# Query loads of 128 rows, a planner that keeps two-input steps apart, narrow zero products and early branch hints in an mLSTM and MoE kernel on one core

## The chip, the cores and the metric

The kernel runs on one core of a Trainium2 chip. The core has five engines with a queue of instructions each, which wait for each other by semaphores: PE (TensorE, matrix products), DVE (VectorE), ACT (ScalarE), POOL (GpSimd) and SP (SyncE), and 16 DMA engines that move data between the chip's memory (HBM) and the core's (SBUF). The metric is the device time of one execution in microseconds (us).

## The reference

Two layers. The first is an mLSTM, a recurrence over 768 tokens for 4 batches and 8 heads of 40 elements; the second a mixture of experts that sends each of the 3072 tokens to one of 8 experts, by its data and its modality.

```python
for t in range(S):                                   # S = 768
    m_new = np.maximum(f_gate[:, :, t] + m, i_gate[:, :, t])
    f_stab, i_stab = np.exp(f_gate[:, :, t] + m - m_new), np.exp(i_gate[:, :, t] - m_new)
    C = f_stab * C + i_stab * outer(v_t, k_t);  n = f_stab * n + i_stab * k_t
    y[:, :, t] = sigmoid(o_gate_t) * (C @ q_t) / np.maximum(np.abs(n @ q_t), 1.0)
x = y as rows of 3072 tokens x 320
logits = x @ w_gate + modality_bias[modality_id]     # 320 x 8
e_idx, gate_w = argmax, its softmax probability
for e in range(8):
    h = np.maximum(x[mask] @ w1[e], 0.0)             # 320 x 1024
    out[mask] = gate_w * (h @ w2[e])                 # 1024 x 320
```

## The kernel before, in words

The kernel has two arms. The first (`still_arm`) assumes properties of the inputs that hold here: that the state of the recurrence is nearly still after the first tokens, and that nearly all tokens of a modality go to one expert. It checks them as it goes, and ends with a verdict (`bword`). A branch on it, L2534, either runs the second, general arm ("rest") or skips it; with these inputs it is skipped. All that follows is the first arm.

**Stages.** The first keys and values (kvs) give a state S for all heads. The 3072 tokens are 24 chunks of 128. For each chunk `light` makes the products S with the chunk's queries (qg), L1924, into the banks Y or H. A query load (`load_q`, L1697) brings two chunks, a gate load (`load_o`, og) the output gates of two. `token_rows` makes tokens of them: DVE multiplies by the gate (xr, L1940), the denominators (ab) follow on ACT, POOL or DVE, POOL divides (L1956), ACT casts the high halves, and DVE or POOL make the low halves (rows, L1610 and L1962). All float32 values are split into two float16 halves, high (h) and low (l), and a product is three products of halves. POOL then scatters the rows into a buffer in HBM, sorted by modality (x_s, L1977).

Two experts, A and B, get all tokens but odd ones. Their weights come in eight pieces each (`load_w`): the load into a stage buffer by SP, the high half by ACT, the low half by DVE (w1lA, w2lA, w1lB, w2lB, L1883). The sorted tokens are 15 tiles, 25 halves of 128 tokens, A and B in turn (`STREAM`). For a tile of two halves, `expert` makes four groups of 16 H products (L2179), which go round three banks (H_63, H_64, H_65); after each, ACT makes hh (the high half after the ReLU, L2184) and DVE hl (L2186), both from the bank. Then follow 24 O products a half (L2195): 16 from hh, 8 from hl. ACT scales them (ob, L2204) and POOL scatters them to the output (L2205). The first tiles' tokens are not taken from HBM but chosen from the rows by products with selection matrices (`select`, sel). `logits` computes the gate of each tile by the real data and finds tokens that go to another expert than their tile's. `odd_row` (L2220 and on) corrects one such token: a product of fs (the sums that tell where it lies) gives fl, from this come its row number fp_i and its expert fe_i; POOL gathers the row (xrow, L2239), SP loads that expert's whole weights into the stage and og buffers, and DVE computes the row by itself (xf, fjunk, facc). The last is summed by a product Y from facc, and scattered.

**What sets the order.** Everything in the arm is a task of `class Plan` (some 1080 tasks): an engine, a duration by formula, what it reads and writes. `plan.run` lays them out in time, each engine taking, of the tasks that are ready, the one with the least latest start time plus a bias; the table `NUDGE` adds a number to the bias of single tasks. A load's end is its issue, then its size by `DMA_KB` behind earlier loads, plus `DMA_FIRST`. The result is only an order: each engine issues its tasks in it, and waits by semaphore for what they need. `idle_products` puts products of a zero tile (zrow) into bank M0 where the plan leaves PE idle over 0.3 us, between 5 and 60 us of planned time.

The instructions of the arm are emitted in two pieces. Between them, on every engine, stands a hint on the branch to "rest", at present ahead of the last tile's O products (`found["cut"]`).

Of the kernel before, what the change touches and what calls it, by code (L numbers as in the profile page):

```python
# [10 lines left out]
F32 = mybir.dt.float32  # L11
# [19 lines left out]
class Plan:  # L31
# [5 lines left out]
    DMA_FIRST = 3.0  # L37
    DMA_KB = 320.0
# [9 lines left out]
    def add(self, eng, dur, fn, r=(), w=(), kb=None, nb=None, chain=None, bias=0.0, lat=0.0):  # L48
# [18 lines left out]
        self.tasks.append(dict(eng=eng, dur=dur, fn=fn, deps=deps, order=order, kb=kb, nb=nb, bias=bias + NUDGE.get(i, 0), lat=lat, early=self.early, w=list(w)))  # L67
# [5 lines left out]
    def run(self):  # L73
# [29 lines left out]
        dma_free = 0.0  # L103
        order, start, end = [], [0.0] * n, [0.0] * n
        while len(order) < n:
# [15 lines left out]
            t = ts[i]  # L121
            start[i] = s
            fin = s + t["dur"]
            e["free"] = fin
# [1408 lines left out]
NSTAGE = 7  # L1533
WARM = 10
FILL = (5.0, 60.0)
PRE = 4
SOON = 20.0
RING = 12
# [41 lines left out]
def still_arm(tc, a, out):  # L1580
# [60 lines left out]
    qg = [tl([120, 2, 3, P], F32, f"qg{i}") for i in range(3)]  # L1641
    qh, ql = ([tl([120, 2, 3, P], F16, f"q{n}{i}") for i in range(2)] for n in "hl")
# [54 lines left out]
    def load_q(i):  # L1697
        dma(368, lambda: sy.dma_start(qg[i % 3], a["ql"][:, 2 * i:2 * i + 2]), w=[f"qg{i % 3}"], bias=FIRST.get(f"q{i}", 0))
# [54 lines left out]
    for h in range(2):  # L1753
        sl = slice(FT * h, FT * h + FT)
        dve(140, lambda sl=sl: v.tensor_tensor_scan(m[:, sl], gf[:, sl], gi[:, sl], -1e30, ALU.add, ALU.max), r=["gs"], w=["m"])
    dve(128, lambda: tt(two(gt)[:, :, 1:], two(gf)[:, :, 1:], two(m)[:, :, 0:FT - 1], ALU.add), r=["gs", "m"], w=["gt"])
# [401 lines left out]
    def expert(k):  # L2158
# [29 lines left out]
        for h in range(nh):  # L2188
            no, op = take("O")
            seq = [(hh, w, f) for f in range(NFC) for w in (w2h, w2l)] + [(hl, w2h, f) for f in range(NFC)]  # L2190
            for q in range(0, 24, 4):
# [8 lines left out]
                if k == len(STREAM) - 1 and q == 0:  # L2200
                    found["cut"] = len(plan.tasks) - 1
# [342 lines left out]
```

## Time and profile before

| | |
|---|---|
| median of 3 runs | 226.71 us (226.43 to 230.26) |
| profiled execution | 226.71 us |
| its span, first to last instruction | 224.9 us |
| granted PE clock, mean | 0.988 |
| PE busy | 207.3 us (92%) |
| DVE, ACT, POOL busy | 139.6, 97.2, 94.9 us |
| HBM read, written | 18.90 MB, 8.47 MB |
| chain that ended last, by engine | PE 58%, DVE 16%, DMA 7%, issue 7%, POOL 4% |

Times in the rows are us from the start of the span unless marked ns. A group's row gives the line, the engine, the operation, what it writes and reads, its count, busy us and mean ns, and behind the bar how long the engine stood idle just before, and what ended that. PEld is the load of a weight tile into PE, which overlaps the products. Line numbers are those of the kernel before; the changed kernel's are 6 to 12 higher.

### The profile page before, as it was taken

What the parts mean: (1) busy time and instruction counts of PE and PEld (TensorE: products, weight loads), DVE (VectorE), ACT (ScalarE), POOL (GpSimd) and SP (SyncE); (2) the same over time, 40 slices, a digit from 0 to 9 for tenths busy, and PEclk for the clock granted to TensorE, in tenths of its full rate; (3) what the DMA queues carried; (4) which work ended last, traced back from release to release, by engine and by line L of the source; (5) the groups of instructions that cost most, each with busy time, mean ns of one, the idle gap of its engine ahead of it and who ended that gap; (6) DMA issues with size and microseconds to landing.
All of it is one profiled execution on the core that took longest, in us unless ns stands there. A gap on an engine that the chain in (4) does not pass through costs nothing.

```text
span 224.9 us, 5443 instructions
## 1 busy us (share of the span) xinstructions
PE 207.3 (92%) x2119; PEld 166.5 (74%) x2119; DVE 139.6 (62%) x396; ACT 97.2 (43%) x200; POOL 94.9 (42%) x122
## 2 busy tenths in 40 slices
PE   7798889699999999979999999999999999999960
PEld 2466768489797887857988878868878788687830
DVE  3869779999689348720596622563316783559940
ACT  2466878376264565430555504223563223134220
POOL 6568789823127716730053873153512040111230
PEclk9999999999999999999999999999999999999995
DMA  6999995959700668255212446510390029500100
GB/s 184 251 360 269 395 354 135 289 178 197 203 29 29 189 165 195 90 146 121 59 61 62 136 147 140 116 44 18 103 164 30 3 80 298 208 28 3 61 5 11
DMA packets 29687, 31.25 MB, mean 139 GB/s; under 512 B 21851, under 2 KB 22397, under 8 KB 29397
## 3 DMA queue, kind: packets, MB, share of 16 engines
q1 hardware_dynamic: 27077, 22.62, 38.6%
q0 software_dynamic: 2432, 8.13, 10.4%
q8 instruction: 18, 0.29, 0.5%
q14 instruction: 16, 0.13, 0.2%
q10 hardware_dynamic: 144, 0.07, 0.1%
HBM read 18.90 MB, written 8.47 MB: 122 GB/s over the span
## 4 chain that ended last, share of the span: by engine, by line
PE 58%; DVE 16%; DMA 7%; issue 7%; POOL 4%; another core or an unknown queue 2%; ACT 2%; SPq 1%; POOLq 0%; DVEq 0%
PE H L2179 29%; PE O L2195 23%; DMA qg<-in_ql 4%; DMA xrow<-x_s,fp_i 3%; PE Y L1924 2%; POOL x_s L1977 2%; DVE w1lA L1883 2%; DVE fjunk L2255 2%; DVE hl L2186 2%; DVE w1lB L1883 1%; ACT hh L2184 1%; PE Y L2039 1%; PE M L2132 1%; DVE w2lA L1883 1%
## 5 line engine op out<-in xcount | busy, mean ns | idle before, releaser
L2186 DVE SCALAR_TENSOR_TENSOR hl<-H,hh 128x512 f16<-128x512 f32 x50 | 34.3, 688 | 43.0 <-ACT hh L2184 38.3
L2205 POOL DMA_INDIRECT out<-ob,ois x25 | 26.3, 1052 | 68.2 <-ACT ob L2204 19.3
L2184 ACT ACTIVATE hh<-H 128x512 f16<-128x512 f32 x50 | 29.7, 597 | 53.4 <-PE H L2179 45.4
L2195 PEld LDWEIGHTS <-hh 128*128 128x128 f16 x400 | 38.0, 98 | 16.8 <-issue 1.8
L2179 PE MATMUL H<-xt,w1hB 128*128 128x256 f16 (+1 forms) x320 | 46.5, 252 | 0.0
L2179 PE MATMUL H<-xt,w1hA 128*128 128x256 f16 (+1 forms) x280 | 43.2, 257 | 0.0
L2179 PE MATMUL H<-xt,w1lB 128*128 128x256 f16 (+1 forms) x192 | 41.4, 252 | 0.0
L2179 PE MATMUL H<-xt,w1lA 128*128 128x256 f16 (+1 forms) x168 | 37.9, 257 | 1.1 <-DVE w1lA L1883 0.6
L1977 POOL DMA_INDIRECT x_s<-rows,pos_i x24 | 27.7, 1154 | 16.8 <-DVE ois L2149 4.8
L2179 PEld LDWEIGHTS <-w1hB 128*128 128x128 f16 x320 | 29.1, 98 | 2.7
L2195 PE MATMUL O<-w2hB,hh 128*128 128x320 f16 x104 | 28.9, 299 | 0.0
L2195 PE MATMUL O<-w2lB,hh 128*128 128x320 f16 x104 | 28.9, 299 | 0.0
L2204 ACT ACTIVATE ob<-O,facs 128x320 f32<-128x320 f32 x25 | 13.1, 527 | 35.0 <-PE O L2195 27.2
L2179 PEld LDWEIGHTS <-w1hA 128*128 128x128 f16 x280 | 25.7, 98 | 2.6
L2195 PE MATMUL O<-w2hA,hh 128*128 128x320 f16 x96 | 26.5, 299 | 1.1 <-ACT hh L2184 1.1
L2195 PE MATMUL O<-w2lA,hh 128*128 128x320 f16 x96 | 26.5, 299 | 1.1 <-DVE w2lA L1883 1.1
L2195 PEld LDWEIGHTS <-hl 128*128 128x128 f16 x200 | 19.0, 98 | 10.2 <-DVE hl L2186 3.1
L2179 PEld LDWEIGHTS <-w1lB 128*128 128x128 f16 x192 | 18.8, 98 | 1.4
L2179 PEld LDWEIGHTS <-w1lA 128*128 128x128 f16 x168 | 16.4, 98 | 2.8 <-DVE w1lA L1883 0.7
L1956 POOL TENSOR_TENSOR xr<-xr,ab 128x640 f32<-128x640 f32 x12 | 15.7, 1307 | 6.3 <-DVE ab L1954 3.4
L2195 PE MATMUL O<-w2hA,hl 128*128 128x320 f16 x96 | 15.5, 299 | 2.1 <-DVE hl L2186 2.1
L2195 PE MATMUL O<-w2hB,hl 128*128 128x320 f16 x104 | 16.6, 299 | 0.0
(199 smaller groups left out, 296.5 us busy)
## 6 DMA issues: line engine op xcount, KB each, us to landing
qg<-in_ql SPq DMA_DIRECT2D x11, 360.0 KB
og<-in_ogl SPq DMA_DIRECT2D x12, 320.0 KB
stage<-in_w1p SPq DMA_DIRECT2D x8, 384.0 KB
stage<-in_w SPq DMA_DIRECT2D x8, 320.0 KB
og<-in_w SPq DMA_DIRECT2D x1, 1280.0 KB
stage<-in_w1t SPq DMA_DIRECT2D x1, 1280.0 KB
kvs<-in_kvs SPq DMA_DIRECT2D x2, 364.5 KB
sp<-in_spq SPq DMA_DIRECT2D x4, 160.0 KB
```

The costliest lines, as they stand in the source:

```text
L1883: dve(n, lambda hi=hi, lo=lo, sv=s3: v.scalar_tensor_tensor(lo, sv, WSC, hi, ALU.mult, ALU.subtract), r=[f"stage{k}", key + "h"], w=[key + ...
L1924: t_.matmul(y[p0:p1, HQ * g:HQ * g + w], lhsT=q[0:k, j, g, p0:p1], rhs=s[0:k, g, 0:w], start=(g == 0 and e == 0), stop=(g == 2 and e == n ...
L1956: lane((320 if lane is dve else 290) * n, lambda z=z, f=f, n=n: f(x4[:, z].rearrange("p c h d -> p (c h) d"), x4[:, z].rearrange("p c h d ...
L1977: ins = g_.indirect_dma_start(out=x_s[:, :], out_offset=bass.IndirectOffsetOnAxis(ap=pos_i[:, c:c + 1].bitcast(U32), axis=0), in_=rows[:, ...
L2039: t_.matmul(y[rs, DV * h:DV * (h + 1)], lhsT=aw[rs, h], rhs=kvs[pr][rs, 9 * D + DV * h:9 * D + DV * (h + 1)], start=(h == 0), stop=(h == H ...
L2179: t_.matmul(hp3[:, i], lhsT=l, rhs=r, start=(i == 0 and q == 0), stop=(i == g - 1 and q == 7), skip_group_check=True)
L2184: act(512, lambda fl=fl, hp3=hp3: s_.activation(hh[:, fl, 0:n], hp3, AF.Relu), r=[nb], w=[f"hh{j}{f}" for f in range(f0, f0 + g)])
L2186: dve(512, lambda fl=fl, hp3=hp3: v.scalar_tensor_tensor(hl[:, fl, 0:n], hp3, 0.0, hh[:, fl, 0:n], ALU.max, ALU.subtract), r=[nb] + [f"hh{ ...
L2195: t_.matmul(op[:, 0:DM], lhsT=t[:, f, P * h:P * h + P], rhs=w[:, f], start=(i == 0), stop=(i == 23))
L2204: act(400, lambda h=h, op=op, o=o: s_.mul(obs[o], op[:, 0:DM], facs[:, s["q0"] + h:s["q0"] + h + 1]), r=[no, f"fac{k}"], w=[f"ob{o}"])
L2205: swdma(164, lambda h=h, o=o: disjoint("outf", g_.indirect_dma_start(out=out[:, :], out_offset=bass.IndirectOffsetOnAxis(ap=ois[:, s["q0"] ...
L2255: dve(420, lambda f=f: v.scalar_tensor_tensor(fjunk, fw1[:, f], 1.0, xf, ALU.mult, ALU.mult, accum_out=fh[:, f:f + 1]), r=["stage0", "xf"] ...
```

## The change

1. The query arrays, in HBM and in SBUF (qg, and the halves qh and ql), have 128 rows and not 120; the last 8 are zero and no product reads them. A load is then 384 KB and not 360. The planner takes 380 KB and not 320 for a microsecond of loads, and 2.7 us and not 3.0 for a load's first bytes.
2. Steps of DVE and POOL that read two SBUF operands are marked (`lk`). The planner starts such a step only when the other engine's last one has ended by plan. No wait is added.
3. Until bank O1 is first written, zero products fill planned gaps of PE over 0.08 us and from 4 us on; they are 128 wide, go to bank O1 and are 0.08 us each by plan. Later they are as before.
4. The arm is cut for the hint where the planned start is 12 us, so the hint stands near the head on each engine.
5. The table `NUDGE` has other numbers, so the order changes in many places.
6. One bound of the verdict's count check is tighter (`LAST`).

```diff
-    DMA_FIRST = 3.0
-    DMA_KB = 320.0
+    DMA_FIRST = 2.7
+    DMA_KB = 380.0
...
+            if t["lk"]:
+                s = max(s, port["POOL" if name == "DVE" else "DVE"] - self.HOP)
             start[i] = s
             fin = s + t["dur"]
+            if t["lk"]:
+                port[name] = fin
...
-FILL = (5.0, 60.0)
+FILL = (4.0, 60.0)
+HINT = 12.0
...
-    qg = [tl([120, 2, 3, P], F32, f"qg{i}") for i in range(3)]
-    qh, ql = ([tl([120, 2, 3, P], F16, f"q{n}{i}") for i in range(2)] for n in "hl")
+    qg = [tl([P, 2, 3, P], F32, f"qg{i}") for i in range(3)]
+    qh, ql = ([tl([P, 2, 3, P], F16, f"q{n}{i}") for i in range(2)] for n in "hl")
...
             dve(n, lambda hi=hi, lo=lo, sv=s3: v.scalar_tensor_tensor(lo, sv, WSC, hi, ALU.mult, ALU.subtract),
-                r=[f"stage{k}", key + "h"], w=[key + "l"])
+                r=[f"stage{k}", key + "h"], w=[key + "l"], lk=True)
...
-        at, fill = 0.0, {}
+        at, fill, fresh = 0.0, {}, True
         for i in order:
             if plan.tasks[i]["eng"] == "PE":
-                if at > FILL[0] and plan.start[i] < FILL[1] and plan.start[i] - at > 0.3:
-                    fill[i] = int((plan.start[i] - at) / 0.25)
+                fresh = fresh and "O1" not in plan.tasks[i]["w"]
+                gap = plan.start[i] - at
+                if at > FILL[0] and plan.start[i] < FILL[1] and gap > (0.08 if fresh else 0.3):
+                    fill[i] = (bank["O1"], P, int(gap / 0.08) + 1) if fresh else (M0, 512, int(gap / 0.25))
                 at = plan.start[i] + plan.tasks[i]["dur"]
...
-    cut = order.index(found["cut"])
...
+    cut = sum(plan.start[i] < HINT for i in order)
+    emit(order[:cut])
     with tc.block():
         tc.mark_branch_hint_location("rest", hint="LikelyTaken", engines=list(nc.engines))
-        with tc.manual_schedule():
-            for i in order[cut:]:
-                plan.tasks[i]["fn"]()
+        emit(order[cut:])
...
-    ql = np.zeros((120, 22, 3, P), np.float32)
+    ql = np.zeros((P, 22, 3, P), np.float32)
```

Where the order changes, at three places of which the prediction speaks. The first is SP's queue at the start, before the change: the keys and values (kvs), then queries (qg) and gates (og); ISA rows are register steps of the weight loads.

```order
L1695 DMA kvs_76<-in_kvs 128x729
L1698 DMA qg_78<-in_ql 120x768
L1701 DMA og<-in_ogl 128x640
L1698 DMA qg_80<-in_ql 120x768
L1698 DMA qg_79<-in_ql 120x768
L1701 DMA og<-in_ogl 128x640 x2
L1857 TENSOR_LOAD e_i
L1857 ISA x2
L1881 ISA
L1881 DMA stage<-in_w 128x640
```

And after it:

```order
L1704 DMA kvs_76<-in_kvs 128x729
L1707 DMA qg_78<-in_ql 128x768
L1710 DMA og<-in_ogl 128x640
L1707 DMA qg_79<-in_ql 128x768
L1710 DMA og<-in_ogl 128x640
L1707 DMA qg_80<-in_ql 128x768
L1710 DMA og<-in_ogl 128x640
L1866 TENSOR_LOAD e_i
L1866 ISA x2
L1890 ISA
```

Queries and gates alternate now, and the second query load (qg_79) comes ahead of the third (qg_80).

The second is PE where the fs product (Y from fs) of the odd row stands. Before, within the O products of the tile ahead (bank O_67, weights of B, from hl):

```order
L2195 MATMUL O_67<-w2hB,hl_113 128x320
L2195 LDWEIGHTS hl_113
L2195 MATMUL O_67<-w2hB,hl_113 128x320
L2229 MATMUL Y_69<-fs_186,ones_f 128x5
L2195 LDWEIGHTS hl_113
L2195 MATMUL O_67<-w2hB,hl_113 128x320
L2195 LDWEIGHTS hl_113
```

And after it, in the O products of the next tile (bank O_66, weights of A):

```order
L2203 LDWEIGHTS hh_110
L2203 MATMUL O_66<-w2hA,hh_110 128x320
L2203 LDWEIGHTS hh_110
L2203 MATMUL O_66<-w2lA,hh_110 128x320
L2235 MATMUL Y_69<-fs_186,ones_f 128x5
L2203 LDWEIGHTS hl_112
L2203 MATMUL O_66<-w2hA,hl_112 128x320
```

It stands behind the sixteen O products from hh of that tile's first half, and ahead of the eight from hl, so behind 64 H products and 20 O products more.

The third is DVE around xf, which reads the gathered row. Here hl_112 is the hl of the same tile (its four groups from the banks H), hl_113 that of the next. Before:

```order
L2186 SCALAR_TENSOR_TENSOR hl_112<-H_64,hh_110 128x512
L2186 SCALAR_TENSOR_TENSOR hl_112<-H_65,hh_110 128x512
L2252 TENSOR_TENSOR xf<-xrow 128x64
L2253 TENSOR_TENSOR xf<-xrow 128x256
L2186 SCALAR_TENSOR_TENSOR hl_112<-H_63,hh_110 128x512
L1970 TENSOR_REDUCE sums<-rows 128x2 x3
L2186 SCALAR_TENSOR_TENSOR hl_113<-H_64,hh_111 128x512
```

And after it, with what comes of the fs product (fl, fe_i, fp_i):

```order
L2194 SCALAR_TENSOR_TENSOR hl_112<-H_63,hh_110 128x512
L2158 SCALAR_TENSOR_TENSOR ois<-fm,ids 128x2
L2158 SCALAR_TENSOR_TENSOR ois<-fm,ids 128x1
L2236 COPY fl<-Y_69 128x5
L2237 TENSOR_SCALAR fe<-fl 128x1
L2238 TENSOR_SCALAR fe_i<-fe 128x1
L2241 TENSOR_SCALAR fe<-fl 128x1
L2239 CAST fp_i<-fl 128x1
L2243 SCALAR_TENSOR_TENSOR fo_i<-fe,fl,pbig 128x1
L1979 TENSOR_REDUCE sums<-rows 128x2 x3
L2258 TENSOR_TENSOR xf<-xrow 128x64
L2259 TENSOR_TENSOR xf<-xrow 128x256
```

Before, fl and fp_i stood ahead of all four hl of the tile, and xf ahead of the fourth; now they stand behind the fourth, and xf ahead of the first hl of the next tile.

More of the change, by code (lines that the diff above doesn't have):

```diff
@@ L46, in __init__, with add @@
         self.early = 0.0
-    def add(self, eng, dur, fn, r=(), w=(), kb=None, nb=None, chain=None, bias=0.0, lat=0.0):
+    def add(self, eng, dur, fn, r=(), w=(), kb=None, nb=None, chain=None, bias=0.0, lat=0.0, lk=False):
         i = len(self.tasks)
@@ L66, in add @@
             self.last_chain[chain] = i
-        self.tasks.append(dict(eng=eng, dur=dur, fn=fn, deps=deps, order=order, kb=kb, nb=nb, bias=bias + NUDGE.get(i, 0), lat=lat, early=self.early, w=list(w)))
+        self.tasks.append(dict(eng=eng, dur=dur, fn=fn, deps=deps, order=order, kb=kb, nb=nb, bias=bias + NUDGE.get(i, 0), lat=lat, early=self.early, w=list(w), lk=lk))
         return i
@@ L103, in run @@
         dma_free = 0.0
+        port = {"DVE": 0.0, "POOL": 0.0}
         order, start, end = [], [0.0] * n, [0.0] * n
@@ L1697, in load_q @@
     def load_q(i):
-        dma(368, lambda: sy.dma_start(qg[i % 3], a["ql"][:, 2 * i:2 * i + 2]), w=[f"qg{i % 3}"], bias=FIRST.get(f"q{i}", 0))
+        dma(393, lambda: sy.dma_start(qg[i % 3], a["ql"][:, 2 * i:2 * i + 2]), w=[f"qg{i % 3}"], bias=FIRST.get(f"q{i}", 0))
     def load_o(i):
@@ L1804, in state @@
             dve(3 * HQ, lambda: v.scalar_tensor_tensor(Sl[b][0:120], Ss[j][0:120], SSC, Sh[b][0:120], ALU.mult, ALU.subtract),
-                r=[f"S{j}{h}" for h in range(3)] + [f"Sh{b}"], w=[f"Sl{b}"])
+                r=[f"S{j}{h}" for h in range(3)] + [f"Sh{b}"], w=[f"Sl{b}"], lk=True)
     modb, sgn, far, ufar = small([NC], "modb", BF16), small([NC], "sgn"), small([NC], "far"), small([NC], "ufar")
@@ L1850, in still_arm @@
                                                      s3[:, :, i:i + 1].broadcast_to([P, 2, E]), ALU.mult),
-            r=["cst", "ss"], w=[("bias", "bt")[i]])
-    pool(40, lambda: g_.tensor_tensor(bias, bias, bt, ALU.add), r=["bt"], w=["bias"])
+            r=["cst", "ss"], w=[("bias", "bt")[i]], lk=True)
+    pool(40, lambda: g_.tensor_tensor(bias, bias, bt, ALU.add), r=["bt"], w=["bias"], lk=True)
     regs = {}
@@ L1963, in token_rows @@
                                                                                rows[:, zc, a0:e0], ALU.subtract),
-                     r=kxr + [f"rowh{c0 + h}" for h in hs], w=[f"rowl{c0 + h}" for h in hs])
+                     r=kxr + [f"rowh{c0 + h}" for h in hs], w=[f"rowl{c0 + h}" for h in hs], lk=True)
         if 2 * i >= RING:
@@ L2389, in still_arm, with emit @@
     order = plan.run()
-    cut = order.index(found["cut"])
     fill = idle_products(order)
-    with tc.manual_schedule():
-        for i in order[:cut]:
-            for _ in range(fill.get(i, 0)):
-                t_.matmul(M0, lhsT=zrow[:, 0:P], rhs=zrow[:, 0:512], start=False, stop=False, skip_group_check=True)
-            plan.tasks[i]["fn"]()
+    def emit(some):
+        with tc.manual_schedule():
+            for i in some:
+                to, w, n = fill.get(i, (M0, 0, 0))
+                for _ in range(n):
+                    t_.matmul(to[:, 0:w], lhsT=zrow[:, 0:P], rhs=zrow[:, 0:w], start=to is not M0, stop=to is not M0, skip_group_check=True)
+                plan.tasks[i]["fn"]()
+    cut = sum(plan.start[i] < HINT for i in order)
+    emit(order[:cut])
     with tc.block():
         tc.mark_branch_hint_location("rest", hint="LikelyTaken", engines=list(nc.engines))
-        with tc.manual_schedule():
-            for i in order[cut:]:
-                plan.tasks[i]["fn"]()
+        emit(order[cut:])
     bad = nc.values_load(bword[0:1, 0:1], min_val=0, max_val=P)
```

65 lines of the change are left out of this document (32 added, 33 removed), and 12 rows, old and new, of the table NUDGE.

## Prediction

> **What bounds the kernel now.** I read the page first, then the windows by stage, then the waits of PE, then the chain of waits, and last the tiles that the change touches. The page's first part says that one engine fills the span, and the windows say where it doesn't. (In each row: length, then busy us of PE, PEld, DVE, ACT and POOL with instruction counts, granted clock, DMA share, GB/s.)
>
> ```profile
> PE 207.3 (92%) x2119; PEld 166.5 (74%) x2119; DVE 139.6 (62%) x396; ACT 97.2 (43%) x200; POOL 94.9 (42%) x122
> ```
> ```profile
> 14.70:20.90 6.20, 5.60 (x46) 3.73 (x45) 6.20 (x11) 4.57 (x10) 5.19 (x6) 1.00 1.04 266
> 20.90:33.00 12.10, 9.80 (x139) 8.56 (x137) 9.21 (x18) 8.90 (x19) 10.06 (x12) 1.00 1.02 379
> 33.00:43.00 10.00, 8.20 (x96) 6.50 (x96) 9.83 (x15) 7.56 (x14) 9.11 (x8) 1.00 0.70 197
> 43.00:60.00 17.00, 17.00 (x230) 14.43 (x230) 15.47 (x48) 8.73 (x17) 4.85 (x9) 1.00 0.91 218
> 200.00:217.30 17.30, 17.30 (x169) 13.39 (x167) 14.93 (x47) 5.54 (x9) 3.14 (x4) 1.00 0.06 21
> 217.30:224.90 7.60, 0.04 (x2) 0.00 (x0) 0.16 (x1) 0.53 (x1) 1.01 (x1) 0.66 0.04 10
> ```
>
> From 43 us on PE is full (17.00 of 17.00, 17.30 of 17.30), and its products there are the same after the change. So time can be won or lost in three places: in the head up to 43 us, at single stalls in the dense part, and in the 7.6 us after PE's last product. In the head PE has products less often than DVE has work: DVE is at 6.20 of 6.20, then 9.21 of 12.10, then 9.83 of 10.00, with POOL close behind. The chain of waits through the head (start, length, what) starts with a load:
>
> ```profile
> 3.14 8.62 DMA qg<-in_ql
> ...
> 11.80 0.91 PE H L1924 x6
> ...
> 15.43 1.35 DVE w2lA L1883
> ...
> 18.45 4.19 DVE w1lA L1883 x3
> ...
> 37.10 3.32 DVE w1lB L1883 x2
> ...
> 42.90 0.72 PE O L2195 x4
> ```
>
> The queries' load releases the lights at 11.80, these release DVE, and from 15.43 to 42.9 DVE's weight halves, with POOL's work between, are what PE waits for. A head that DVE begins earlier, with as much work, ends as much earlier.
>
> **The queries' 128 rows.** A query load and a weight piece hold rows of the same length; this is the rate in 40 slices of 0.4 us from 4 to 20 us, with the sizes from the page:
>
> ```profile
> GB/s 200 356 243 224 221 297 323 236 227 213 250 251 242 266 234 236 245 252 394 402 381 415 385 412 385 403 394 378 369 330 200 214 250 259 227 278 239 258 217 269
> qg<-in_ql SPq DMA_DIRECT2D x11, 360.0 KB
> stage<-in_w1p SPq DMA_DIRECT2D x8, 384.0 KB
> ```
>
> Slices 3 to 17 (5.2 to 11.2 us) average 248 GB/s: the query loads, with one og load between. Slices 18 to 27 carry og and weights of 128 rows, at 395. Six microseconds at 248 are 1.49 MB. With three times 24 KB more and at 395 they take 3.95 us, so the loads behind stand 2.05 us earlier. The second stretch at such a rate, slices 30 to 39, holds the next two query loads: 720 KB (0.74 MB) at its mean of 241 take 3.06 us, 768 KB at 395 take 1.99, another 1.07. Together that is a lead of 3.1 us. It could be 0, if the slow rate comes from the source and not from the row count; I take 395, since og's rows, also cut out of a wider array, reach it.
>
> [...]
>
> What does DVE make of the lead? The wait of PE for the query load and the length of the lights:
>
> ```profile
> PE O L2195 <- DVE hl L2186: 1.8, 2, 1.1
> PE H L1924 <- DMA qg<-in_ql: 1.5, 1, 1.5
> ```
> ```profile
> L1924 PE MATMUL H<-S,qg x12: 241/275/372, 11.8 to 13.1; 120*128 120x123 f32 x8, 80*128 80x82 f32 x4
> ```
>
> Twelve products, the lights of one query load, run from 11.8 to 13.1 us, so the three loads' lights need 3.9 us in any order. Only the wait of 1.5 us in front of them goes, so DVE's first weight half starts about 1.5 to 2 us earlier. Its later waits follow the loads:
>
> ```profile
> L1883 DVE SCALAR_TENSOR_TENSOR w2lA<-stage,w2hA x4: 760/817/1435, 15.3 to 32.2; 128x640 f16<-128x640 f32 x4
> L1883 DVE SCALAR_TENSOR_TENSOR w1lA<-stage,w1hA x4: 945/953/2453, 18.4 to 25.2; 128x768 f16<-128x768 f32 x4
> L1883 DVE SCALAR_TENSOR_TENSOR w1lB<-stage,w1hB x4: 948/1570/2296, 34.4 to 42.8; 128x768 f16<-128x768 f32 x4
> ...
> DMA stage<-in_w1p: 1.4, 1
> ```
>
> Between 20.9 and 33 the DMA engines are full (1.02), and DVE waits 1.4 us for a weight piece. With the loads 3.1 us ahead, that wait shrinks until DVE is 3.1 ahead as well. I put the lead at PE's dense start at 3.1, with 1.5 and 3.6 as ends.
>
> **Two-input steps kept apart.** The rule adds no wait; it only moves steps in the plan. The same w1l half takes 945 ns or 2453 ns. Excess over the fastest is 0.7 us for w2lA at most once, and about 4 us over the eight w1 halves (1.5 at most for the slow one of A, 0.6 times four for B by its median). Against POOL's work beside it:
>
> ```profile
> L1977 POOL DMA_INDIRECT x_s<-rows,pos_i x9 | 12.4, 1381 | 3.1 <-issue 1.6 <-DVE rows L1610 0.7 <-POOL rows L1962 0.6
> L1956 POOL TENSOR_TENSOR xr<-xr,ab 128x640 f32<-128x640 f32 x5 | 6.8, 1363 | 3.3 <-DVE ab L1954 1.8 <-DVE rows L1987 1.5
> ```
>
> POOL and DVE are busy 19.2 and 19.0 of the 22.1 us from 20.9 to 43, so they must overlap most of the time; the scatters, 12.4 us, are not under the rule at all. I take 0.7 of the 4.7, with ends of -0.5 (the plan meets other collisions) and 2.5.
>
> **Narrow zero products** stand between the lights and before them, where PE waited.
>
> ```profile
> 7.76 0.82 PE L2395 MATMUL M<-zrow 128*128 128x512 f16 x3
> ```
>
> Three of 512 columns take 0.82, so eight of a quarter of that width take at most 0.55, if they cost by width. They stand before the last group of lights, whose load now is there before PE comes; DVE has a weight half in front of what these lights feed, which hides them. I count nothing; without that cover it is 0.55.
>
> **Branch hints.** The branch after the verdict is followed by 3.9 us in which SP waits, and the last scatter is issued behind it.
>
> ```profile
> SPq L2534 <- SPq L2534: 3.9, 1, 3.9
> ```
> ```profile
> 218.24 1.01 POOL L2205 DMA_INDIRECT out<-ob,ois  x1 [0.97 <-ACT ob L2204]
> ```
>
> The scatter ends at 219.25 and the span at 224.9; 5.65 us lie between. A hint that holds can take part of SP's 3.9; one given 200 us ahead may be worthless by then, and PE and DVE, which had theirs near the end, lose it. No row shows either, so I bound it by -1.5 and +1 and take -0.5. [...]
>
> **What moves late.** One product that decides an odd token's row, Y from fs, moves on PE from the end of one tile's O products to behind sixteen O products of the next. The special row's transfer (xrow) hangs on it, and in DVE's queue xf, which reads that transfer, stands in front of an hl. Now xf stands one hl later.
>
> ```profile
> 181.43 0.28 PE L2229 MATMUL Y<-fs,ones_f 128*128 128x5 f32 x2
> ```
> ```profile
> 191.27 0.98 PE L2195 MATMUL O<-w2hA,hl 128*128 128x320 f16 x6
> 192.56 0.45 PE L2195 MATMUL O<-w2hA,hl 128*128 128x320 f16 x2 [0.31 <-DVE hl L2186]
> ```
> ```profile
> 183.54 7.71 DMA xrow<-x_s,fp_i
> ...
> 191.34 0.22 DVE xf L2252
> ...
> 196.26 5.25 PE H L2179 x48
> ```
> ```profile
> 198.68 0.69 DVE L2186 SCALAR_TENSOR_TENSOR hl<-H,hh 128x512 f16<-128x512 f32 x1 [4.00 <-ACT hh L2184]
> ...
> 200.42 0.69 DVE L2186 SCALAR_TENSOR_TENSOR hl<-H,hh 128x512 f16<-128x512 f32 x1 [0.33 <-ACT hh L2184]
> ...
> 202.17 0.69 DVE L2186 SCALAR_TENSOR_TENSOR hl<-H,hh 128x512 f16<-128x512 f32 x1 [0.33 <-ACT hh L2184]
> ...
> 203.94 0.68 DVE L2186 SCALAR_TENSOR_TENSOR hl<-H,hh 128x512 f16<-128x512 f32 x1
> ```
>
> The seventeenth O product ran at 191.27, where the fs product will stand: 9.84 us later than at 181.43. On POOL the gather now stands behind one output scatter more, whose data are ready long before, and SP's two loads follow the same product as before, so the transfer lands 9.84 later too, at 201.1 on before's clock, and xf, which ended 0.56 behind the landing (191.34 and two steps), at 201.65. The hl behind it was begun at 198.68, and would be at 198.4 without PE's stall of 0.31: 3.3 us late. PE's H groups go round three banks, so the fourth group wants the bank that this hl frees. It comes there at 196.26 + 5.25 - 0.31 = 201.2 and now gets it at 202.3, a stall of 1.1. The four hl with the sums between them took 5.9 us (198.68 to 203.94, and 0.6 of the last); two waits of 0.33 go, and one step of the odd row (an eighth of fjunk, 0.5) now stands ahead of the fourth, so it ends at 207.4. PE reaches O at 204.05 and the twenty-third product, which wants it, some 3.1 later (0.14 a product, from six in 0.98), at 207.15: another 0.25. Less the 0.31 that goes, PE is 1.05 late. DVE is still 1.2 behind PE then, with 14.93 busy of 17.3 us and the verdict at its end; between 0 and 1.2 of that reaches the end, and I put 0.45. I take +1.5 in all. Ends: -0.3, if the transfer is quicker and only the stall goes, and +5.8, worked out under (d).
>
> **The sum.** Against the profiled execution: 224.9 of span - 3.1 - 0.7 - 0.5 + 1.5 = 222.1. That execution took 226.71, 1.8 outside its span, and is itself the median of the runs shown. So 223.9.
>
> **Rivals.**
> (a) The gains come in full and late work is hidden: 3.1 + 2.0 of collisions + 1.2 after the branch + 0.3 at the late stall, 226.7 - 6.6 = 220.1. For it: the collisions hold 4.7. Against: POOL's load, and xf's place. 0.19.
> (b) DVE and POOL keep the head, and the loads' lead ends in new waits for POOL's scatters and bias: 1.5 stays of it, and 0.7 is lost elsewhere with +1.5 late: 226.7 - 1.5 + 0.7 + 1.5 - 0.5 = 226.9. For it: POOL is at 9.11 of 10.00 before 43 us, and its scatters are not shortened. 0.16.
> (c) The change does not do what it says: the slow rate belongs to where the queries lie, and a load of 128 rows is as slow. No lead, 0.7 of collisions, late +1.5, tail -0.5: 227.0. Against it stands the 395 of og. 0.06.
> ```profile
> og<-in_w SPq DMA_DIRECT2D x1, 1280.0 KB
> stage<-in_w1t SPq DMA_DIRECT2D x1, 1280.0 KB
> ```
>
> (d) Slower: xrow's transfer. In the 7.71 us that it took, two loads of weights for the odd row, 2.62 MB, released by the same fs product, went over the same engines; at 395 GB/s these alone are 6.6 us. At 241 they are 10.9, the transfer lands 4.3 later, the bank stall is 5.4 and not 1.1, and the late term is +5.8. With the rest as forecast that is 226.7 - 3.8 - 0.5 + 5.8 = 228.2; with a head lead of 1.5 alone and the hint lost (+1), 232.0. It decides from a late term of 4.3, a landing at 203.9 on before's clock. 0.07.
>
> **Numbers.** The forecast case, 221.6 to 226, has 0.52. The range shall leave out 2 in 10: the lower half of (a), the upper halves of (b) and (c), and (d): 220.0 to 227.3. Two per cent, about what can be told from no change here, is 222.2 and 231.3. Below 222.2 lie (a) and 0.11 of the forecast case: 0.30. Above 231.3 lies half of (d), and a little that I have not thought of: 0.05. Within: 0.65.
>
> **What would show it.** Right: lights of all three query loads in one run from 8.7 us, the rate near 395 from 5.2 us on; w2lA's first half before 13.5; PE dense from 39 to 40; DVE waiting for xrow some 3 us in front of an hl, and PE for an H bank or hl behind it. SP's wait after the branch under 3.9 if the hint holds. Wrong: slices still at 250 while queries load; w1 halves above 1.5 us as often as now; PE's head stalls moved to hl and not gone; a stall late of over 2 us, or none.

## The result: 228.47 us, 1.1% slower, where 223.9 was forecast

The changed kernel took 228.47 us (median of 19 runs, 227.34 to 230.74), the kernel before 227.86 on the same chip (19 runs, 224.27 to 230.26): a ratio of 1.011, 95% interval 1.008 to 1.014. This ratio counts fast runs alone, which are all 19 of the changed kernel but, of the kernel before, only the nine within 1.5% of its fastest; by the medians of all runs it is 1.003. So the change is less than 2% slower; by neither count is there the gain of 1.2% that was forecast. The profiled execution took 229.12 us, its span is 227.3.

The windows by stage after the change (columns as in the prediction), and behind them two windows of the middle, which the prediction didn't look at, first after, then before:

```profile
14.70:20.90 6.20, 5.22 (x39) 3.02 (x38) 5.29 (x12) 5.21 (x12) 3.40 (x4) 1.00 1.04 396
20.90:33.00 12.10, 9.14 (x130) 8.45 (x129) 9.55 (x16) 7.44 (x17) 11.01 (x11) 1.00 0.96 286
33.00:43.00 10.00, 10.00 (x121) 8.28 (x120) 9.45 (x17) 7.44 (x13) 8.60 (x10) 1.00 0.51 139
...
75.00:92.00 17.00, 15.78 (x159) 12.70 (x157) 9.90 (x27) 8.60 (x20) 8.61 (x10) 1.00 0.68 183
92.00:106.00 14.00, 12.07 (x102) 9.73 (x101) 5.99 (x12) 4.42 (x8) 6.01 (x6) 1.00 0.48 120
...
220.60:227.30 6.70, 0.02 (x2) 0.00 (x0) 0.16 (x1) 0.53 (x1) 1.00 (x1) 0.89 0.05 11
```
```profile
75.00:92.00 17.00, 17.00 (x173) 14.06 (x171) 9.59 (x21) 9.63 (x20) 8.56 (x10) 1.00 0.67 173
92.00:106.00 14.00, 12.86 (x107) 10.10 (x105) 3.82 (x7) 3.09 (x6) 4.89 (x5) 1.00 0.52 143
```

PE is dense from 33 us on, ten earlier than before. But it is idle for 1.22 us between 75 and 92 and for 1.93 between 92 and 106, where before it lost 1.14 in all. Adding up the stretches that no row of PE covers, its zero products left out, the 2.4 us between the two spans are: head, up to 60 us, 1.20 less time without a product (15.88 to 14.68); the products themselves, most of it the first ones at a lower pace, 1.82 more; stalls from 60 to 200 us, 1.56 more; the stall behind the odd row, 1.08 more; the end behind PE's last product, 0.9 less. So in this execution the head is 0.6 slower on balance; the low pace at its start isn't the change's, as the last section shows.

The loads did what was forecast. The rate in slices of 0.4 us from 4 to 20 us, after, then what the DMA engines had moved in that window, after and before:

```profile
GB/s 168 223 291 292 268 351 379 356 335 405 384 430 401 405 417 417 408 352 329 378 352 332 273 338 410 425 391 406 395 411 358 376 404 416 407 433 376 376 393 388
```
```profile
DMA packets 2473, 5.86 MB, mean 366 GB/s; under 512 B 408, under 2 KB 424, under 8 KB 2472
```
```profile
DMA packets 1975, 4.63 MB, mean 289 GB/s; under 512 B 353, under 2 KB 369, under 8 KB 1975
```

By 20 us 1.23 MB more have come, which at 395 GB/s are 3.1 us: the lead of the prediction. For what PE and DVE made of it, the profiled execution is a poor witness, since its first products ran at the low pace. Its first lights start at 9.85 us, where before they start at 8.70. In a_same, the same program at the pace of the kernel before, they start at 8.81. Its first and last group of lights, and the weight halves of DVE, first w2lA in a_same, then all three in the profiled execution:

```profile
8.81 1.57 PE L1933 MATMUL H<-S,qg 120*128 120x123 f32 x12 [0.58 <-DVE S L1619]
...
12.10 1.61 PE L1933 MATMUL Y<-S,qg 120*64 120x123 f32 x18
```
```profile
L1892 DVE SCALAR_TENSOR_TENSOR w2lA<-stage,w2hA x4: 761/815/818, 13.2 to 29.4; 128x640 f16<-128x640 f32 x4
```
```profile
L1892 DVE SCALAR_TENSOR_TENSOR w2lA<-stage,w2hA x4: 760/814/818, 14.6 to 30.8; 128x640 f16<-128x640 f32 x4
L1892 DVE SCALAR_TENSOR_TENSOR w1lA<-stage,w1hA x4: 896/947/2316, 18.0 to 25.7; 128x768 f16<-128x768 f32 x4
L1892 DVE SCALAR_TENSOR_TENSOR w1lB<-stage,w1hB x4: 890/946/1097, 32.5 to 38.1; 128x768 f16<-128x768 f32 x4
```

The lights of the three loads now run from 8.81 to 13.71 with one pause of 0.38 us; before they ran from 8.70 to 14.75 with a wait of 1.53 for a load. DVE's first weight half starts 2.1 us earlier than before (13.2 for 15.3), about as forecast, and the first low halves of the rows, from which PE's selection products are made, 0.9 earlier (15.79 for 16.70, a_same and before):

```profile
15.79 0.88 DVE L1619 SCALAR_TENSOR_TENSOR rows<-xr,rows 128x128 f16<-128x128 f32 x2
```
```profile
16.70 0.88 DVE L1610 SCALAR_TENSOR_TENSOR rows<-xr,rows 128x128 f16<-128x128 f32 x2
```

DVE doesn't keep that lead. Before, it waited 1.7 us for ACT's gates and 1.4 for a weight piece in the head. Both waits are gone, but at 27.8 us DVE now waits 2.54 us for the denominators (ab) that POOL makes behind two scatters; POOL's rows and DVE's, in the profiled execution:

```profile
27.59 1.06 POOL L1986 DMA_INDIRECT x_s<-rows,pos_i  x1 [0.16 <-issue]
28.96 0.98 POOL L1986 DMA_INDIRECT x_s<-rows,pos_i  x1 [0.30 <-issue]
29.96 0.31 POOL L1962 TENSOR_SCALAR ab<-ab 128x16 f32<-128x16 f32 x1
```
```profile
30.30 0.25 DVE L1963 RECIPROCAL ab<-ab 128x16 f32<-128x16 f32 x1 [2.54 <-POOL ab L1962]
```

In a_same the same wait of 2.54 us stands at 26.3.

SP's wait behind the branch and the last scatter, after:

```profile
SPq L2546 <- SPq L2546: 0.5, 1, 0.5
```
```profile
221.51 1.00 POOL L2211 DMA_INDIRECT out<-ob,ois  x1 [0.97 <-ACT ob L2210]
```

The scatter ends at 222.51, 4.79 us before the span does; that was 5.65.

### The profile page after: what moved, and what is told of

Its sections match the earlier page's. It is cut to its first block, busy times and chain, and to the rows that moved or that the text cites. A ratio compares the mean times of both kernels' runs of the same rounds, so it can differ in the third digit from the quotient of the medians.

```text
span 227.3 us, 5475 instructions
## 1 busy us (share of the span) xinstructions
PE 210.7 (93%) x2140; PEld 169.9 (75%) x2140; DVE 140.6 (62%) x396; ACT 97.1 (43%) x200; POOL 94.6 (42%) x122
## 4 chain that ended last, share of the span: by engine, by line
PE 68%; issue 14%; DMA 5%; DVE 4%; POOL 2%; another core or an unknown queue 1%; ACT 1%; SPq 1%; POOLq 1%; DVEq 0%; ACTq 0%
PE H L2187 32%; PE O L2203 27%; DMA stage<-in_w1p 3%; DMA og<-in_ogl 2%; PE Y L1933 2%; PE O L1722 2%; POOL out L2211 2%; DVE w1lA L1892 1%; PE M L2141 1%; PE Y L2033 1%; PE Y L2048 1%; SPq L1890 1%; DVE w2lA L1892 1%; POOLq L2396 1%
## 5 line engine op out<-in xcount | busy, mean ns | idle before, releaser
L2187 PE MATMUL H<-xt,w1hA 128*128 128x256 f16 (+1 forms) x280 | 43.7, 257 | 0.0
L1986 POOL DMA_INDIRECT x_s<-rows,pos_i x24 | 27.2, 1134 | 14.5 <-issue 4.5
L2187 PEld LDWEIGHTS <-w1hA 128*128 128x128 f16 x280 | 25.2, 98 | 2.6
L2203 PE MATMUL O<-w2hA,hl 128*128 128x320 f16 x96 | 15.3, 299 | 0.0
```

Source lines behind the costliest of these rows:

```text
L1986: ins = g_.indirect_dma_start(out=x_s[:, :], out_offset=bass.IndirectOffsetOnAxis(ap=pos_i[:, c:c + 1].bitcast(U32), axis=0), in_=rows[:, ...
L2187: t_.matmul(hp3[:, i], lhsT=l, rhs=r, start=(i == 0 and q == 0), stop=(i == g - 1 and q == 7), skip_group_check=True)
L2203: t_.matmul(op[:, 0:DM], lhsT=t[:, f, P * h:P * h + P], rhs=w[:, f], start=(i == 0), stop=(i == 23))
```

## The experiments

Eighteen runs followed, in five sets, each set on one chip beside the kernel before; three of them (a_same, a_same2, a_same3) are the changed kernel as it is. a_noout1 and a_zero leave out part of the result. The table gives the ratio to the kernel before, its 95% interval, and PE's idle time from 75 to 110 us in the profile (35 us less the busy time of that window; a dash where it wasn't read).

| run | chip | ratio | interval | PE idle 75–110 |
|---|---|---|---|---|
| before / after (first pair) | not listed | 1.011 | 1.008–1.014 | 1.14 / 3.16 |
| b_rows | 2 | 0.991 | 0.988–0.994 | 0 |
| a_wide | 2 | 0.990 | 0.987–0.993 | 0 |
| a_late | 2 | 0.985 | 0.982–0.988 | 0 |
| b_hint | 2 | 0.999 | 0.995–1.003 | 0 |
| a_same | 12 | 1.009 | 1.005–1.014 | 3.17 |
| a_120 | 12 | 1.023 | 1.016–1.030 | 3.24 |
| a_hintlate | 12 | 1.010 | 1.005–1.016 | – |
| b_rows_gmin | 12 | 0.996 | 0.991–1.001 | 1.19 |
| a_same2 | 7 | 1.004 | 1.001–1.007 | 2.59 |
| a_wide2 | 7 | 1.004 | 1.000–1.008 | 2.59 |
| a_late2 | 7 | 1.004 | 1.001–1.007 | – |
| b_rows_hint | 7 | 1.000 | 0.996–1.004 | 1.06 |
| a_same3 | 6 | 1.007 | 1.003–1.012 | 2.67 |
| a_noout1 | 6 | 0.996 | 0.991–1.001 | 0 |
| a_gap | 6 | 0.993 | 0.989–0.996 | 0 |
| a_zero | 6 | 1.009 | 1.005–1.012 | 2.66 |
| b_gap | 0 | 1.000 | 0.996–1.004 | 0 |
| a_gap_late | 0 | 0.985 | 0.980–0.990 | 0 |

**The parts one by one.** b_rows is the kernel before with the rows alone:

```diff
-    qg = [tl([120, 2, 3, P], F32, f"qg{i}") for i in range(3)]
-    qh, ql = ([tl([120, 2, 3, P], F16, f"q{n}{i}") for i in range(2)] for n in "hl")
+    qg = [tl([P, 2, 3, P], F32, f"qg{i}") for i in range(3)]
+    qh, ql = ([tl([P, 2, 3, P], F16, f"q{n}{i}") for i in range(2)] for n in "hl")
...
-    ql = np.zeros((120, 22, 3, P), np.float32)
+    ql = np.zeros((P, 22, 3, P), np.float32)
```

> The kernel before with query loads of 128 rows and nothing else; plan and order are before's. If the loads' lead is worth what the prediction said, the lights' wait for qg (1.5 us) goes and the time falls by 1.5 to 3.1 us (ratio to before 0.987 to 0.993). The rival: the lights' wait goes, but DVE, ACT and POOL set the head, so the stalls of PE before its dense part keep their sum (16.2 us up to 43) and the ratio is 0.997 to 1.003. The slices between 5.2 and 11.2 us should show near 395 GB/s in both cases; at 250 the row count would not be the cause of the rate.

It gained 0.9%, 1.9 us by the medians (226.94 to 225.02), as the first of the two expected cases has it. a_120 is the reverse, the changed kernel with 120 rows in the same three lines.

> The changed kernel with query loads of 120 rows: order, planner, fills and hint are the change's. If the row count is worth in this order what b_rows showed in before's (2 us), the time is 1.5 to 2.5 us above the changed kernel's. If the change's order gets more of the lead than before's order did (its first weight half starts at 13.7 us and not at 14.7), it is 2.5 to 4 us above. The rival: the lead is lost in both orders alike, and the difference is under 1 us.

Against a_same, the changed kernel unchanged in the same set, it lost 1.35% (1.0227 against 1.0092). Its rate from 4 to 20 us shows why:

```profile
GB/s 146 214 202 280 294 228 291 224 227 238 221 248 210 193 269 236 247 243 221 242 188 234 265 319 408 401 373 399 419 394 399 377 375 375 387 386 354 370 301 285
```

Nothing but the row count differs, and from 5.2 to 13.2 us the loads come at 240 GB/s on average again, where a_same has 366. So it is the row count that makes the rate here; why it does, no run shows.

How much of it PE gets hangs on the order. In the changed order it gets all: up to 60 us PE's time without real products is 17.42 us in a_120 and 14.37 in a_same, 3.05 less, and the medians lie 3.2 us apart (232.63 and 229.47). That is the second of the expected cases. In the old order it gets little: from the kernel before to b_rows that time fell by 0.46 us (15.88 to 15.42). The 1.9 us of the medians aren't in this profile, which is of an execution 1.0 us above b_rows's median. The chain of waits through its head (start, length, what):

```profile
7.86 0.81 POOL sel L2093
...
9.69 0.72 POOL sel L2093
...
10.46 0.11 POOL gmin L1715
...
10.59 0.92 ACT gjunk L1891 x2
...
12.30 0.49 DVE xr L1940
...
14.81 1.35 DVE w2lA L1883
```

No load stands in it any more: three selection masks on POOL, a memset behind them, ACT's check of the gates behind that, and only then the steps that lead to DVE's weight half. b_rows_gmin moves that memset ahead of the third mask by one entry, `19: -400`, in the table of b_rows.

> The kernel before with 128 rows (b_rows) and one table entry more: the 0.1 us memset of gmin on POOL stands ahead of the third sel and not behind it, so ACT's check of the gates (gjunk) runs ahead of its first ab. In b_rows the lights end 1.6 us earlier than before, but DVE's first weight half only 0.6: DVE waits for ACT's gates, ACT for gmin, POOL makes sel. If the lead was lost there, w2lA's first half starts 0.6 to 0.9 us earlier than in b_rows (14.7 us) and the time falls by 0.3 to 0.9 us more (ratio to before 0.987 to 0.990). The rival: the next of POOL's and DVE's steps takes the place and the ratio stays at 0.991.

The weight half began at 14.42 and not 14.73, and the time without real products up to 60 us fell by the same 0.3 us (15.42 to 15.11). The ratio, 0.996, was measured on a chip with stalls in the middle, and so doesn't stand beside b_rows.

b_hint is the kernel before with the cut of the hint at 12 us of planned time; a_hintlate the changed kernel with before's cut.

```diff
-    cut = order.index(found["cut"])
+    cut = sum(plan.start[i] < 12.0 for i in order)
```

> The kernel before with the branch hint where the planned start is 12 us; all else is before's. If the early hint holds, the end behind the last scatter shrinks as in the change (from 5.65 to 4.8 us) and SP's wait behind the branch from 3.9 to 0.5: ratio 0.995 to 0.998. The rival: what shrank there came from elsewhere, the early hint is worth nothing, and the ratio is 1.000 to 1.004.

> The changed kernel with the branch hint where before had it, ahead of the last tile's O products. If the early hint is worth 0.85 us as b_hint's profile says (4.8 us from the last scatter's end to the end of the span, against 5.6), the time is 0.6 to 1.0 us above the changed kernel's and SP again waits some 3.9 us behind the branch. The rival: no difference.

The end behind the last scatter was 4.8 us in b_hint as in the changed kernel; without the early hint it had been 5.65 in the kernel before. In the whole time that isn't to be measured (0.999; 1.010 beside 1.009).

a_wide is the changed kernel with the zero products of before (wide, in planned gaps over 0.3 us from 5 us on).

> The changed kernel with zero products by before's rule (512 wide into M0, none before 5 us of plan); order and hint are the change's. In the changed kernel's trace the products from kvs run at 0.2 us apart where before they run at 0.1, and PE's products only double their pace at 10.8 us (before: 4.4), and the first light starts 1.15 us later. If the narrow products are the cause, the pace doubles before 6 us here and the time falls by 1 to 1.6 us against the change (ratio to before 1.004 to 1.007). The rival: when the pace doubles has nothing to do with these products, and the ratio stays at 1.011.

a_late takes six late entries of the table back, so that the fs product and xf stand where they stood:

```diff
-    781: 10, 788: -77, 808: -24, 813: -1, 860: 8, 927: 20, 936: 13, 938: -16, 944: -13, 948: 34, 1072: 47,
+    781: 10, 788: -77, 808: -24, 813: -7, 936: 13, 938: -16, 944: 14, 948: 9,
```

> The changed kernel with six entries of the table for the end of the plan put back to before's (860, 927, 813, 1072, 944, 948): the fs product stands again ahead of the last four O products of the tile before, and xf ahead of the fourth hl; the plan up to 169 us is the change's. If the late row costs what the prediction said, DVE's wait of 6.6 us for xrow and PE's stall of 1.4 us behind it go, and the time falls by 1.0 to 2.0 us against the change (ratio to before 1.002 to 1.007). The rival: the stall is made up for elsewhere and the ratio stays at 1.009 to 1.012.

Both seemed to cure the change: 0.990 and 0.985. But they ran on another chip than the changed kernel had, and there no kernel had a stall in the middle. So three went side by side, with the rows and the early hint together on the old order as a fourth:

> The changed kernel once more, beside the kernel before. In its first profile PE lost 3.2 us between 83 and 103 us in waits for ACT (before: 1.1 at 99 us), and no kernel with the change's or before's order has such waits in the four profiles since; its first lights ran at half pace. If these two belong to that occasion and not to the change, the time here is between a_wide's and before's: ratio 0.988 to 0.998, with the stall of 1.2 to 1.4 us behind xrow still there. The rival: the change itself is slower, and the ratio is again 1.008 to 1.014.

> The changed kernel once more, now beside its own two variants on one chip. Theory A (the order itself costs it: the stalls between 81 and 104 us, 1.6 us more than before, and the stall behind the last tile's odd rows): 1.005 to 1.014 of before again, and 1.5 to 2.5% above the variants with the wide zero products and with the late entries taken back. Theory B (those stalls belong to the chip on which the earlier pair was measured, not to the order): the three within 0.7% of one another, whatever the ratio to before is.

> The changed kernel with the zero products of before (wide, from 5 us). Theory A: 0.99 of before as it was, with no stall of PE over 0.4 us between 80 and 105 us. Theory B: within 0.7% of the unchanged changed kernel beside it, and the same stalls as it or none in both.

> The changed kernel with the six late entries of the table taken back (product of the last flags and the last tile's features at before's places). Theory A: 0.985 of before, 1.5 to 2.5% under the changed kernel; of that no more than 0.9% (about 2 us) can come from the places after 190 us, the rest from the stretch between 81 and 104 us. Theory B: 0.2 to 0.9% under the changed kernel, all of it after 190 us.

> The kernel before with two parts of the change alone: queries with 128 rows and the branch hint at 12 us. If the parts add up: 0.991 x 0.999 = 0.990 of before, some 2.2 us less; the stretch from the last scatter's end to the end of the span 4.8 us instead of 5.6. If the early hint also moves the head's code, the gain of 0.9% of the rows is partly lost: 0.993 to 0.998.

The first three gave 1.004: neither the zero products nor the late entries had cured the change, and the same two variants stand below 1 on chip 2 and above it on chip 7. b_rows_hint came to 1.000, with 1.06 us of stall. I had read the first set as a story of the edits, and that story fell.

**The stall in the middle.** ACT's rows of the changed kernel, its PE rows around the stall, and how the kernel before had shown the same in its chain of waits:

```profile
98.78 0.60 ACT L2192 ACTIVATE hh<-H 128x512 f16<-128x512 f32 x1 [2.41 <-PE H L2187]
102.01 0.60 ACT L2192 ACTIVATE hh<-H 128x512 f16<-128x512 f32 x1 [2.63 <-remote]
```
```profile
98.83 0.27 PE L2187 MATMUL H<-xt,w1lA 128*128 128x256 f16 x1
...
102.66 0.31 PE L2203 MATMUL O<-w2hA,hh 128*128 128x320 f16 x1 [1.93 <-ACT hh L2192]
```
```profile
94.81 4.37 another core or an unknown queue
```

The last product of the fourth H group ends at 99.10 by its row, and ACT, idle, begins on it at 102.01. PE's signal came at 101.99, 2.89 us after the end shown. Then PE waits for hh. In a_wide on chip 2, an idle ACT begins 0.04 us after the end of such a group (94.80 for 94.76). In every trace with this stall, and in none from chips 2 and 0, the groups of two stretches (near 79 and 97 us) are signalled late: by up to 3.0 us in the changed order; in the old one by up to 1.7 in the first stretch and 3.3 in the second, where ACT begins at 99.20 on a group that ends at 95.89. What stands there on POOL is a train of scatters, in the changed kernel six with 0.3 us between them:

```profile
74.17 1.54 POOL L1986 DMA_INDIRECT x_s<-rows,pos_i  x1 [0.17 <-issue]
76.02 0.98 POOL L1986 DMA_INDIRECT x_s<-rows,pos_i  x1 [0.30 <-issue]
...
79.85 0.97 POOL L2211 DMA_INDIRECT out<-ob,ois  x1 [0.31 <-issue]
81.13 0.97 POOL L2211 DMA_INDIRECT out<-ob,ois  x1 [0.30 <-issue]
```

In the old order the first train has five, since the second result scatter comes 5 us later; the second train has six as well. Two theories: the trains hold the signals up (S), or PE's own pace falls in long runs of dense products, unseen in the granted clock, which reads 1.00 (P). With a_same3 as the control: a_noout1 leaves out the two result scatters of tile 4, a_gap puts three memsets ahead of each of four such scatters, a_zero feeds the products with zeros.

```diff
-            swdma(164, lambda h=h, o=o: disjoint("outf", g_.indirect_dma_start(
+            swdma(164, lambda h=h, o=o: None if k == 4 else disjoint("outf", g_.indirect_dma_start(
```
```diff
+    junk = tl([P, 768], F32, "junk")
...
+            swdma(164, lambda h=h, o=o: (k in (4, 5) and [g_.memset(junk, 0.0) for _ in range(3)], disjoint("outf", ...
```
```diff
                     for q, (l, r) in enumerate(ops):
+                        r = zrow[:, 0:n] if q and k >= 3 else r
...
-                        t_.matmul(op[:, 0:DM], lhsT=t[:, f, P * h:P * h + P], rhs=w[:, f], ...
+                        t_.matmul(op[:, 0:DM], lhsT=t[:, f, P * h:P * h + P], rhs=zrow[:, 0:DM] if i and k >= 3 else w[:, f], ...
```

> The changed kernel once more, as the control for the three beside it. If this chip shows the stalls of TensorE at 82 to 87 and 100 to 103 us (together 2.6 to 3.2 us): 1.004 to 1.011 of before. If it does not: 0.985 to 0.992, as its two variants were where no stall showed.

> The changed kernel without the two scatters of results that close the first train on GpSimd (those of the tile called 4; its rows of the output are left out), so that four scatters stand in a row at 72 to 77 us instead of six; the second train at 91 to 98 us keeps its six. Theory S (the trains of scatters hold the signals up): the stall at 82 us goes (0.6 to 0.75 us), the one at 100 us (1.4 to 1.9 us) stays; 0.5 to 1.2 us under the control. Theory P (TensorE's own pace): both stalls as in the control, time within 0.3 us of it.

> The changed kernel with three memsets of 128x768 (together some 2 us) on GpSimd ahead of each of the four scatters of results in the two trains (tiles 4 and 5), so that no train is longer than four. Theory S: both stalls shrink, the first to nothing, the second to under 1 us; 1 to 2 us under the control, 1.000 or less of before. Theory P: both stay, time as the control or up to 0.5 us over it.

> The changed kernel with the products of the expert layers from tile 3 on fed with zeros: all but the first of a group's products read zeros as their moving side, so that the data that toggles in TensorE is nearly all gone, and the instructions stay the same in number, shape and order (the experts' results are left out). Theory S: the stalls at 82 and 100 us stay as in the control. Theory P, where the pace falls by power: both go, and the time is 2 to 3 us under the control.

The windows of the middle, first of the control, then of a_gap, and POOL and ACT in a_gap:

```profile
75.00:92.00 17.00, 15.85 (x160) 12.77 (x158) 9.99 (x29) 8.43 (x21) 8.87 (x10) 1.00 0.69 183
92.00:106.00 14.00, 12.48 (x106) 10.02 (x104) 5.98 (x12) 4.60 (x8) 6.01 (x6) 1.00 0.46 119
```
```profile
75.00:92.00 17.00, 17.00 (x173) 14.04 (x171) 11.26 (x31) 9.84 (x22) 13.20 (x16) 1.00 0.76 183
92.00:106.00 14.00, 14.00 (x119) 11.39 (x118) 5.70 (x9) 3.58 (x7) 11.15 (x12) 1.00 0.46 119
```
```profile
78.68 0.98 POOL L1987 DMA_INDIRECT x_s<-rows,pos_i  x1 [0.30 <-issue]
79.64 2.37 POOL L2212 MEMSET junk<- 128x768 f32 x3
82.17 0.97 POOL L2212 DMA_INDIRECT out<-ob,ois  x1 [0.16 <-issue]
```
```profile
95.95 0.60 ACT L2193 ACTIVATE hh<-H 128x512 f16<-128x512 f32 x1 [1.15 <-PE H L2188]
97.70 0.60 ACT L2193 ACTIVATE hh<-H 128x512 f16<-128x512 f32 x1 [1.15 <-PE H L2188]
```

Twelve memsets that do nothing, four times 2.4 us of POOL's time, make the kernel 3.6 us faster (225.15 against 228.79): PE is at 31.00 of the two windows' 31.00, and ACT gets a group every 1.75 us. With zeros both stalls stay (2.66 us idle, 2.67 in the control), and so does the ratio (1.009 beside 1.007), so P falls, as far as the pace would hang on the data. a_gap did what S says, and more. In a_gap and a_noout1 no H group beside the trains is signalled more than 0.23 us late, so POOL's scatters there are the place. But S as stated missed once: in a_noout1 the second train's stall went too, though its six scatters were all there, and the gain was 2.4 us where 0.5 to 1.2 were expected. Its second scatter there took 1.35 us and not 0.98, so this train was not the same either; why that was enough, I can't say. That the length of a train by itself makes the signals late is therefore not shown.

Last, the gaps alone on the kernel before, and the gaps with the late entries taken back; both edits as shown:

> The kernel before with three memsets of 128x768 on GpSimd ahead of each of the four scatters of results of tiles 4 and 5, as in the changed kernel with gaps. Its own stall at 98 to 100 us (1.1 us) should go: 0.995 of before (0.992 to 0.998). If it is 0.990 or less, the gain of the gaps has nothing to do with the change's order; if 0.998 or more, the old order did not need them, and the stall there has another cause.

> The changed kernel with the gaps and with the six late entries of the table taken back. No stall between 80 and 105 us. The stall behind the last tile's odd rows (0.9 to 1.4 us at 200 to 204 us) is replaced by one near 191 us of up to 1.6 us, and the end after the last scatter is some 1 us shorter, as in the earlier run: 0.986 to 0.993 of before. If it is 0.993 or more, the late entries cost nothing by themselves.

b_gap gained nothing, but on a chip that, as the next paragraph has it, is of the kind without late signals; so it doesn't tell what the old order would gain on the others. a_gap_late took 223.11 us, a ratio of 0.985, the same as a_late on the other chip of that kind. There the gaps had nothing to cure, and cost nothing. a_gap beats both kernels on a chip with late signals, and a_gap_late on one without; a_gap_late on a chip with them wasn't run.

**What stays open.** The same trains cost nothing on chip 2: a_wide has six scatters from 73.14 to 81.06 us, one every 1.3 us, and not a late signal. The traces differ there in one more thing. The completion records of the DMA transfers stand on sixteen semaphores, 16 a transfer where all are there (in the kernel before, 16 between 13.62 and 13.95 us on one of them), and its 137 transfers would leave 2192 (135 leave 2160 in a_noout1). They number 2136 to 2161 in all six traces from chips 2 and 0, and 1672 to 1769 in the other fourteen (1697 before, 1689 after): there a fifth or a little more is missing. Late signals stand only among the latter. All times here are of recorded executions, so the recording may have a part in the stall, and a kernel run unrecorded might show none; that is a guess, and no run tells it apart from the chip.

## Why the prediction was wrong, step by step

**The lead of the loads (-3.1): the step that failed first.** The lead itself came to 3.1 us, and DVE began 2.1 us earlier, about as forecast. What failed is "A head that DVE begins earlier, with as much work, ends as much earlier", and with it the lead of 3.1 at PE's dense start. The forecast took DVE's later waits to follow the loads. The wait of 1.4 us for a weight piece went, but a wait of 2.54 us for POOL's denominators, behind two scatters, came in the new order. In b_rows, too, the chain goes through POOL's masks, a memset and ACT and not through a load. PE became dense at 33 us and not at 39 to 40, but part of its idle time had only moved ahead: it has no product but zero ones for 3.29 us from 15.15 on, where before the longest such stretch was 2.32. In all, PE's time without a real product up to 60 us is 14.3 to 15.7 us in the traces of the changed order with 128 rows (a_zero aside), and 15.9 to 16.2 in those of the old order with 120: a gain of 0.2 to 1.8 us (1.20 in the first pair), where 3.8 were summed.

That is rival (b) in its kind. It had the new waits for POOL's scatters and left 1.5 of the lead. The sum also had no term for the new order in the head. a_120 has one: with 120 rows the new order needs 17.42 us there and the old 15.88, so the new order has more to gain from the rows (3.05) and without them is worse by 1.5. The two parts don't add up one by one, and which entry of the table does it wasn't run.

**The stalls in the middle: the term that was missing.** "Single stalls in the dense part" was named as a place where time is lost, but only the late one was priced. The row of 4.37 us put down to an unknown queue stood in the chain before. I didn't follow it, and so didn't ask what a longer train of scatters would do to it. It is worth 2.0 us between 75 and 110, more than the head gained in the first pair; with the trains broken up, the change is 0.7% faster than before and not 0.7% slower, on one chip. The changed kernel as it is never ran on a chip without late signals. a_wide, the nearest to it there, has 0.990, close to the forecast's 0.988. But its head gained only 0.9 us against b_hint on the same chip (15.91 to 14.99), so that this nearness is luck in part.

**Collisions (-0.7).** The excess over the fastest fell by about 3 of the 4.7 us: w1lB's median went from 1570 to 946 ns, w2lA's worst from 1435 to 818, one w1lA of 2316 is left. That is more than forecast. In b_rows, with the old order, they stay as they were (1570 and 1427 ns), so the new order did it; no run takes the rule out by itself, and none shows PE gaining by it. That POOL's steps beside them are what lengthens a half was the forecast's assumption; no run shows it.

**Narrow zero products (0).** a_wide2 equals a_same2. Right.

**The hint (-0.5).** 0.86 in the trace (from 5.65 to 4.79 us behind the last scatter, SP's wait from 3.9 to 0.5), although the hint is given 200 us ahead: right in kind. The size was a choice between bounds that no row gave, so that it came near is luck, and in the whole time it can't be told.

**The late step (+1.5): right in its mechanism.** The fs product ran at 193.1, and DVE waited for the transfer ahead of an hl, and PE for the bank (rows of ACT, DVE and PE):

```profile
199.54 0.60 ACT L2192 ACTIVATE hh<-H 128x512 f16<-128x512 f32 x1 [1.17 <-PE H L2187]
```
```profile
203.18 0.23 DVE L2258 TENSOR_TENSOR xf<-xrow 128x64 f32<-128x64 f16 x1 [6.58 <-DMA xrow<-x_s,fp_i]
...
203.65 0.68 DVE L2194 SCALAR_TENSOR_TENSOR hl<-H,hh 128x512 f16<-128x512 f32 x1
```
```profile
204.39 0.38 PE L2187 MATMUL H<-xt,w1hB 128*128 128x256 f16 x2 [1.39 <-DVE hl L2194]
```

That is 1.39 for the forecast 1.1, and against the 0.31 before 1.08 for 1.05; the 0.45 put on top of it for the end isn't seen. DVE stood idle for 6.58 us, but this hl had its input from ACT only at 200.14, so it came 3.5 us late, for the forecast 3.3. The old places cost as much, once PE comes sooner; PE's row in a_late:

```profile
192.49 0.45 PE L2203 MATMUL O<-w2hA,hl 128*128 128x320 f16 x2 [1.60 <-DVE hl L2194]
```

So taking the step back is no cure by itself, and a_late2 was no faster than a_same2.

**The range.** 220.0 to 227.3 rests on these terms. By the prediction's own chances it leaves out 0.28 and not the 2 in 10 that it names. The variants that compute the whole result and show no stall in the middle fell inside it, 223.1 to 225.2; the change itself lies 1.2 above.

## What to carry to other kernels

Follow every piece of a chain that a profile puts down to an unknown source, above all where an order moves DMA issues together: what came with the scatters of POOL, which is busy for 42% of the span, cost more in the first pair (2.0 us) than the whole head gained (1.20). A load that came earlier was worth only what the later inputs allowed, here POOL's denominators, for which DVE waited 2.54 us. So the worth of a faster load hangs on the order around it, 0.5 us of PE's time in the old one and 3.05 in the new. And compare variants only beside each other on one chip: ratios to a common reference differed by up to 2% between chips and told a false story for a while.

## What the runs showed that I had not expected

The first products ran at a lower pace in some executions, whatever the kernel; the products of the state, first in the profile of the changed kernel, then in a_same, which is the same program:

```profile
L1798 PE MATMUL H<-kvs,kw x12: 407/408/558, 6.6 to 8.4; 64*120 64x123 f32 x12
```
```profile
L1798 PE MATMUL H<-kvs,kw x12: 262/265/363, 6.3 to 7.2; 64*120 64x123 f32 x12
```

The granted clock reads 1.00 in both. b_hint, with the wide zero products, had the slow pace too (median 410 ns), a_wide had not (265), so the kind of zero products doesn't decide it. In the profiled execution these products took 2.15 us and not 1.21, and the first lights 1.97 and not 1.57. So what its head shows is read beside a_same.

PE's signals came up to 3.3 us behind the ends shown, in the first pair and on chips 12, 7 and 6, beside trains of five or six scatters, one every 1.3 us. With gaps of 2.4 us ahead of the last two of a train, at most 0.22 us was left there.
